# A fused linear-attention and ELU-MLP kernel: order of ScalarE work at the end of the first unit, and plain products in the second unit's first pairs

## The chip, the cores and the metric

The kernel runs on one core of a Trainium2 chip. A core has a matrix engine (TensorE, PE), three engines for elementwise work (VectorE, DVE; ScalarE, ACT; GpSimd, POOL), and SyncE (SP), which issues most transfers. Each engine works through its own instruction list in order and waits at semaphores for the others. The metric is device microseconds of one execution; the median of three timed runs counts.

## The reference

Two stages are computed in float32. The first is a gated linear attention: for each of 4 batches and 8 heads a state of 48 by 48 is decayed and updated at each of 768 positions, and the output is the query times the state. The second is a two-layer MLP with an ELU over all 3072 tokens; d_model is 384 and d_ff 2048.

```python
f = 1.0 / (1.0 + np.exp(-f_logit))
for t in range(S):
    state = f[:, :, t, :, None] * state + np.einsum('bhd,bhe->bhde', k[:, :, t], v[:, :, t])
    y[:, :, t] = np.einsum('bhd,bhde->bhe', q[:, :, t], state)
h = x @ w_in                                   # x: y with the heads side by side
g = np.where(h > 0.0, h, np.exp(np.minimum(h, 0.0)) - 1.0)
return g @ w_out
```

The weights arrive as float64 and are brought to float32 on the chip.

## The kernel before, in words

The tokens are cut into 12 *units* of 256 (`U`); d_ff is cut into 8 *pairs* (`NP`) of two 128-wide tiles. A program step is numbered `T`; there are 16 steps in a unit, two in a pair. In an even step `up(P)` forms the hidden activations of pair P, and in an odd step `down(P - LAG)`, two pairs behind, multiplies the finished activations by `w_out` and adds them up in PSUM. P counts through all units, so pairs 0 to 7 belong to unit 0, and pairs 8 to 15 to unit 1. What else happens in a step (attention of later units, weights, blends) is registered with `at_step(T, ...)` and emitted before the step's `up` or `down`; `later` holds work emitted at the end of a step. The whole order is written out by hand, so each engine's list is the order in which the Python code emits instructions. This driver is the loop at the end of `fast`, and the registrations stand just before it.

Unit 0 is *direct*: `up` is 6 matmuls of 256 columns into one PSUM buffer of the tag "h" (L946), and `down` 4 matmuls of 384 columns (L978). From unit 1 on (`m >= DIRECT`) both are Strassen-like products of 2 by 2 blocks with seven block products in place of eight. `up7` (L901) takes two "h" buffers, `pa` and `pb`; there are two in all. Its combined weights are made by `mix` (L882) and its combined inputs by `blend` (L889), both on POOL. `down` needs sums of the activations, four POOL operations for each pair, made in `elu` (L965), and differences of `w_out` blocks, `combos`, made by the generator `combine` on VectorE (L869), one operation for each step from step `CB` on; its matmuls are 192 columns wide (L1003). At the end of a unit VectorE puts four PSUM banks together into the output (L1013, L1014).

The ELU of a direct pair: `exped` has ScalarE do Relu and Exp from PSUM (L933, L934); `elu` has VectorE do the rest (L955), still reading the pair's PSUM buffer, which is free only after that. For a seven-product pair ScalarE copies one block (`u1`, L908), VectorE adds it to two others (L910, which frees `pa`), and `joined` does three further adds (L923, which free `pb`) before Relu and Exp.

Weights: part n arrives in one of seven slots of `area`, VectorE splits it (`split`, L567, L571), ScalarE lowers the lower half (`lower`, L577), and VectorE merges both into float32 (`merge`, L585). Parts 14 and 15 are the last two parts of `w_out`. `combos` lie in slots of `area` that have been emptied by then.

Attention of unit 2: `gates(2)` (L616, L618) is two ScalarE operations over the forget gates; `decays` (L630 scan, L635 reciprocal, both on VectorE, then scaling by POOL at L625) follow in steps 16, 18 and 20, and `settle` in step 22. `warm(0, "a0", MORE)` emits `MORE` matmuls of one by one element (L1058) in step 22. Unit 0's result is copied from PSUM to SBUF by ScalarE (L985) in step 19; unit 1's `down` writes over the same banks from step 21 on.

Of the kernel before, what the change touches and what calls it, by code (L numbers as in the profile page):

```python
# [17 lines left out]
def general(  # L18
# [38 lines left out]
    PAD = 64 - D  # L57
    LAG = 2
    HALF = (slice(0, D), slice(64, 64 + D))
# [297 lines left out]
def fast(ctx: ExitStack, tc: tile.TileContext, q, k, v, f_logit, w_in, w_out, out, flag, outer):  # L357
# [30 lines left out]
    NFT = DFF // 128  # L388
    NKT = DM // 128
    PAD = 64 - D  # L390
    NP = NFT // 2
    DH = DM // 2
    DIRECT = 1
    LAG = 2
    AHEAD = 7
    WA = 1
    F1 = 3
    W0 = 3
    SMALL = 16
    MORE = 5  # L400
    RR = 2
    HOLD = 2
    A1 = (2, 8, 10, 11)
# [3 lines left out]
    A3 = (2, 5, 9, 11)  # L407
    BL = 13
    MX = 10
    CB = 16  # L410
    BL1 = 13
    LIMIT = 2.0**80

# [103 lines left out]
    if wide:  # L517
        combos = [area[:, i].bitcast(FP32).rearrange("p (n f) -> p n f", f=DH) for i in (5, 6, 0, 1)]
    else:
        apart = cst.tile([128, 4, NP, DH], FP32, name="combos")  # L520
        combos = [apart[:, i] for i in range(4)]
# [7 lines left out]
    order = [divmod(i, NP) for i in range(NU * NP)]  # L529
# [3 lines left out]
    needs = sorted(  # L533
        (2 * P + out_ * (2 * LAG + 1), j, out_) for P, (m, j) in enumerate(order) if m == 0 for out_ in range(2)
    )
# [37 lines left out]
    def lower(n):  # L573

        if wide and n < NFT:
            raw = raws[n]
            nc.scalar.activation(raw.bitcast(U16)[:, 2::4], raw.bitcast(U32)[:, 0::2], AF.Copy, scale=2.0**-29)  # L577
# [33 lines left out]
    def gates(u, pieces=(NKT,), bias=1):  # L611

        p = 0
        for n in pieces:
            a = qkf[u % NB]["f"][:, p : p + n, 0]
            nc.scalar.activation(a, a, AF.Exp, scale=-1.0)  # L616
            if bias:
                nc.scalar.activation(a, a, AF.Copy, bias=1.0)  # L618
            p += n
# [210 lines left out]
    plan, later = {}, {}  # L830

    def at_step(step, *todo):
        plan.setdefault(step, []).extend(todo)
# [25 lines left out]
    gs, ss, pms, phs = {}, {}, {}, {}  # L859

    def combine():

        b = [[wo[:, i::2, h * DH : (h + 1) * DH] for h in range(2)] for i in range(2)]
        t = combos
        for n in range(0, NP, 2):
            for to, x, y in (
                (t[0], b[0][1], b[0][0]), (t[1], b[1][1], t[0]), (t[2], b[1][1], b[0][1]), (t[3], b[1][0], t[1]),
            ):
                nc.vector.tensor_tensor(  # L869
                    out=to[:, n : n + 2], in0=x[:, n : n + 2], in1=y[:, n : n + 2], op=ALU.subtract  # L870
                )
                yield
# [18 lines left out]
    def up7(P):  # L891
# [19 lines left out]
        add(h[:, 0:2], pa[:, 1:3], u1[:].unsqueeze(1).broadcast_to([128, 2, 128]))  # L911
        if order[P - 1][0] >= DIRECT:
            elu(P - 1)
# [23 lines left out]
    def up(P):  # L937

        m, j = order[P]
        if m >= DIRECT:  # L940
            up7(P)
# [10 lines left out]
    def elu(P):  # L952
        m, j = order[P]
        g = gs[P]
        nc.vector.scalar_tensor_tensor(  # L955
            out=g[:], in0=g[:], scalar=-1.0, in1=phs.pop(P), op0=ALU.add, op1=ALU.max
        )
        if m >= DIRECT:
            s = ss[P] = sb.tile([128, 4, 128], FP32, tag="sums", name=f"sums{m}_{j}", bufs=3)
            a = [[g[:, i, t * 128 : (t + 1) * 128] for i in range(2)] for t in range(2)]  # L960
            for i, x, y, op in (
                (0, a[1][0], a[1][1], ALU.add), (2, a[0][0], a[1][0], ALU.subtract),
                (1, s[:, 0], a[0][0], ALU.subtract), (3, a[0][1], s[:, 1], ALU.subtract),
            ):
                nc.gpsimd.tensor_tensor(out=s[:, i], in0=x, in1=y, op=op)  # L965
# [3 lines left out]
    def down(P):  # L969
        m, j = order[P]  # L970
        if j == 0:
            pms[m] = [ps.tile([128, DM], FP32, tag=f"m{i + (m < DIRECT)}", name=f"psM{m}_{i}") for i in range(NW if m < DIRECT else 4)]
        pm, g = pms[m], gs.pop(P)
        ends = dict(start=(j == 0), stop=(j == NP - 1))
        if m < DIRECT:
            for i in range(2):
                for t in range(NW):
                    nc.tensor.matmul(  # L978
                        pm[t][:], lhsT=g[:, i, t * 128 : (t + 1) * 128], rhs=wo[:, 2 * j + i, :],
                        start=(j == 0 and i == 0), stop=(j == NP - 1 and i == 1),  # L980
                    )
            if j == NP - 1:
                o = (outer if (NU - m) % 2 else sb).tile([128, 2, DM], FP32, tag="o", name=f"o{m}", bufs=1)
                for t in range(NW):
                    nc.scalar.copy(o[:, t], pm[t][:])  # L985
                    t0 = m * U + t * 128
                    nc.sync.dma_start(out=out[t0 : t0 + 128, :], in_=o[:, t])
                del pms[m]
            return
        s = ss.pop(P)  # L990
        a = [[g[:, i, t * 128 : (t + 1) * 128] for i in range(2)] for t in range(2)]
        b = [[wo[:, 2 * j + i, h * DH : (h + 1) * DH] for h in range(2)] for i in range(2)]
        c = [combos[i][:, j] for i in range(4)]

        todo = [
            (0, 0, a[0][0], b[0][0]), (3, 0, a[0][1], b[1][0]), (0, 1, s[:, 1], c[1]),
            (1, 0, s[:, 0], c[0]), (1, 1, s[:, 2], c[2]), (2, 1, a[1][1], c[3]), (2, 0, s[:, 3], b[1][1]),
        ]
        if j == 0:
            todo = todo[3:] + todo[:3]  # L1000
        for bank, half, x, y in todo:
            first = j == 0 and (bank, half) in ((0, 0), (3, 0), (1, 0), (2, 1))
            nc.tensor.matmul(  # L1003
                pm[bank][:, half * DH : (half + 1) * DH], lhsT=x, rhs=y,
                start=first, stop=(j == NP - 1), skip_group_check=True,
            )
        if j == NP - 1:
            p = [[pm[i][:, h * DH : (h + 1) * DH] for h in range(2)] for i in range(4)]
            o = (outer if (NU - m) % 2 else sb).tile([128, 2, DM], FP32, tag="o", name=f"o{m}", bufs=1)
            u2 = sb.tile([128, DH], FP32, tag="u2", name=f"u2_{m}", bufs=1)  # L1010
            u43 = sb.tile([128, 2, DH], FP32, tag="u43", name=f"u43_{m}", bufs=1)
            flat = o[:].rearrange("p t f -> p (t f)")
            add = lambda to, x, y: nc.vector.tensor_tensor(out=to, in0=x, in1=y, op=ALU.add)  # L1013
            (nc.vector.tensor_copy if m == NU - 1 else nc.scalar.copy)(u2[:], p[0][0])  # L1014
            add(flat[:, 0:DH], p[3][0], u2[:])
            add(u2[:], p[0][1], u2[:])
            add(u43[:], pm[1][:].rearrange("p (h f) -> p h f", h=2), u2[:].unsqueeze(1).broadcast_to([128, 2, DH]))
            add(flat[:, 3 * DH :], p[1][0], u43[:, 1])
            add(flat[:, DH : 3 * DH], pm[2][:], u43[:].rearrange("p h f -> p (h f)"))
            def store(*queues):  # L1020
                for t in range(2):
                    for h in ((1, 0) if t else (0, 1)):
                        queues[t].dma_start(
                            out=out[m * U + t * 128 : m * U + (t + 1) * 128, h * DH : (h + 1) * DH],
                            in_=o[:, t, h * DH : (h + 1) * DH],
                        )

            if m == NU - 1:
                left.append(store)
            else:  # L1030
                store(nc.sync, nc.sync)
            del pms[m]
# [70 lines left out]
    a = qkf[1]["f"][:, 0:NKT, 0]  # L1103
# [36 lines left out]
    scale(1, ("q", 1, nc.gpsimd), ("q", 2, nc.gpsimd))  # L1140
    at_step(A1[2], lambda: outputs(1), lambda: lower(A1[2]), lambda: lower(A1[2] + 1))
    for n in range(1, NFT):
        t = min(max(needs[n][0] - 2, 0), n)
        at_step(t, lambda n=n: merge(n))
        if n > 1:
            later.setdefault(max(t - 2, 0), []).append(n)
    at_step(F1, lambda: move(1, 1, nc.scalar))
    at_step(F1 + 2, lambda: scale(1, ("q", NKT, nc.gpsimd)))
    at_step(A1[0], lambda: transposed(1, 0, "a0"), lambda: transposed(1, 1, "a1"))
# [1 line left out]
    at_step(22, lambda: warm(0, "a0", MORE))  # L1151
    attention(1, (), A1)
    at_step(8, lambda: load(2))
    at_step(14, lambda: gates(2))
    attention(2, D2, A2)
    weights = combine()
    for n in range(NFT):
# [5 lines left out]
    for u in range(3, NU):  # L1163
        t = (u - 1) * NFT
# [5 lines left out]
    for n in range(NR):  # L1170
        t = 3 * NFT + (NU - 4) * NFT * n // NR + RR
# [4 lines left out]
    for T in range(NU * NFT):  # L1176
        P = T // 2
        sevens = order[P][0] >= DIRECT
        if T % 2 and sevens:
            joined(P)  # L1180
        if T % 2 == 0 and P and order[P - 1][0] < DIRECT:
            elu(P - 1)
        for f in plan.pop(T, ()):
            f()
        if T % 2 == 0:
            up(P)
        elif P >= LAG and T not in joint:
            if T - 2 in joint:
                down(P - LAG - 1)
            down(P - LAG)  # L1190
        for n in later.pop(T, ()):
            split(n)
            if n not in (A1[2], A1[2] + 1):
                lower(n)
    elu(NU * NP - 1)
    for P in range(NU * NP - LAG, NU * NP):
# [51 lines left out]
```

## Time and profile before

| what | value |
|---|---|
| three runs | 562.26, 562.70, 563.56 us; median 562.7 |
| profiled execution | 563.12 us, of which the span from first to last instruction is 561.4 |
| TensorE busy | 542.9 us, 97% of the span |
| TensorE weight loads | 507.9 us, 90% |
| VectorE busy | 407.5 us, 73% |
| ScalarE busy | 228.1 us, 41% |
| GpSimd busy | 293.3 us, 52% |
| mean granted TensorE clock | 0.995 of full speed |

All times of a trace are counted from the span's start. A matmul in float32 appears as two records, each with its own weight load; records overlap, so the distance from start to start tells the rate rather than the duration. A line of a timeline gives start, duration of the stretch, engine, line of the code, operation, output and inputs, shapes and the count; in square brackets stands the idle time before it and what ended it. In a list of waits, a line gives who waited, for whom, and then the sum in us, the number of times and the longest.

### The profile page before, as it was taken

To read this page: it belongs to the slowest core of one execution; us is meant where nothing else is said; L and a number is where in the kernel's file an instruction comes from. 1 tells how busy PE (TensorE), PEld (TensorE's weight loads), DVE (VectorE), ACT (ScalarE), POOL (GpSimd) and SP (SyncE) were. 2 spreads that over 40 slices of the span, in tenths; PEclk is the share of its full clock that TensorE was granted. 3 is DMA by queue.
4 is the path that set the end of the run, shared out by engine and by line. 5 is a ranking of instruction groups with operands and counts; after the bars stand their busy time and mean duration, and the time that the engine had idled before them with its cause. 6 is when DMAs were issued, how large, how long until landed. Compare 5 with 4: busy or idle time off the path is not lost.

```text
span 561.4 us, 15627 instructions
## 1 busy us (share of the span) xinstructions
PE 542.9 (97%) x6358; PEld 507.9 (90%) x6358; DVE 407.5 (73%) x804; ACT 228.1 (41%) x442; POOL 293.3 (52%) x567
## 2 busy tenths in 40 slices
PE   6889989999999999999999999999999999999996
PEld 2466768999999999999999999999999999999995
DVE  8888989786675785785785785786687777735553
ACT  3288752443343434434344343343333343333331
POOL 6600797475375375465366267257258348325332
PEclk9999989999999999999999999999999999999999
DMA  8999971024025216207307307207307302301101
GB/s 198 233 266 247 276 184 43 3 48 123 2 48 149 61 26 182 77 18 189 81 9 189 87 10 190 85 9 191 86 9 185 93 9 71 87 5 33 31 2 34
DMA packets 39474, 54.30 MB, mean 97 GB/s; under 512 B 4032, under 2 KB 29216, under 8 KB 39392
## 3 DMA queue, kind: packets, MB, share of 16 engines
q1 hardware_dynamic: 38592, 52.61, 36.3%
q8 instruction: 52, 0.85, 0.6%
q10 hardware_dynamic: 800, 0.59, 0.5%
q14 instruction: 30, 0.25, 0.2%
HBM read 45.02 MB, written 4.72 MB: 89 GB/s over the span
## 4 chain that ended last, share of the span: by engine, by line
PE 85%; DMA 7%; DVE 3%; ACT 2%; issue 1%; SPq 1%; POOL 0%; ACTq 0%; DVEq 0%; POOLq 0%
PE psH L901 39%; PE psM L1003 36%; DMA area<-in_moe_w_in_dram 5%; DMA area<-in_moe_w_out_dram 2%; PE psY L751 2%; PE psY L771 2%; PE psU_a L736 2%; PE psS L713 2%; ACT area L577 1%; PE psT L673 1%; PE psM L978 1%; DVE bits L567 1%; DVE gg L955 0%; DVE wi L585 0%; DVE state L694 0%
## 5 line engine op out<-in xcount | busy, mean ns | idle before, releaser
L901 PE MATMUL psH<-xt,wi 128*128 128x128 f32 (+1 forms) x1056 | 195.9, 295 | 0.0
L965 POOL TENSOR_TENSOR sums<-gg 128x128 f32<-128x128 f32 x176 | 77.6, 462 | 209.6 <-DVE gg L955 190.9
L933 ACT ACTIVATE gg<-hh 128x512 f32<-128x512 f32 x88 | 55.5, 631 | 252.9 <-DVE hh L923 111.9
L901 PEld LDWEIGHTS psH<-xt,wi 128*128 128x128 f32 x1056 | 150.1, 192 | 1.6
L901 PE MATMUL psH<-xt,area 128*128 128x128 f32 x704 | 122.0, 275 | 2.0 <-DVE gg L955 2.0
L901 PEld LDWEIGHTS psH<-xt,area 128*128 128x128 f32 x704 | 106.9, 192 | 6.8 <-DVE gg L955 2.2
L910 DVE TENSOR_TENSOR hh<-psH,u 128x256 f32<-128x256 f32 x88 | 37.0, 421 | 99.6 <-ACT u L908 99.6
L1003 PE MATMUL psM<-area,sums 128*128 128x192 f32 x528 | 102.1, 326 | 0.1
L1003 PEld LDWEIGHTS psM<-area,sums 128*128 128x128 f32 x528 | 88.0, 190 | 0.2 <-issue 0.2
L1003 PE MATMUL psM<-wo,gg 128*128 128x192 f32 x352 | 73.9, 332 | 0.0
L955 DVE SCALAR_TENSOR_TENSOR gg<-gg,hh 128x512 f32<-128x512 f32 x88 | 63.3, 720 | 1.5 <-ACT gg L934 1.5
L635 DVE RECIPROCAL f<-f 128x256 f32<-128x256 f32 x36 | 62.8, 1747 | 1.1
L934 ACT ACTIVATE gg<-gg 128x512 f32<-128x512 f32 x96 | 60.5, 631 | 3.0
L1003 PEld LDWEIGHTS psM<-wo,gg 128*128 128x128 f32 x352 | 56.3, 190 | 1.4
L923 DVE TENSOR_TENSOR hh<-psH,u43h 128x256 f32<-128x256 f32 (+1 forms) x176 | 54.7, 353 | 3.0
L965 POOL TENSOR_TENSOR sums<-gg,sums 128x128 f32<-128x128 f32 x88 | 46.8, 532 | 6.9
L625 POOL TENSOR_TENSOR q<-q,f 128x256 f32<-128x256 f32 x48 | 39.7, 829 | 18.1 <-DMA area<-in_moe_w_in_dram 15.1
L625 POOL TENSOR_TENSOR k<-k,f 128x256 f32<-128x256 f32 x48 | 39.7, 830 | 9.5 <-DMA f<-f 6.7
L923 DVE TENSOR_TENSOR u43h<-psH,hh 128x256 f32<-128x256 f32 x88 | 37.0, 421 | 9.2 <-PE psH L901 8.5
L965 POOL TENSOR_TENSOR sums<-sums,gg 128x128 f32<-128x128 f32 x88 | 43.4, 493 | 0.0
L1003 PE MATMUL psM<-area,gg 128*128 128x192 f32 x176 | 43.0, 326 | 0.0
L1003 PE MATMUL psM<-wo,sums 128*128 128x192 f32 x176 | 43.0, 326 | 0.0
(100 smaller groups left out, 648.7 us busy)
## 6 DMA issues: line engine op xcount, KB each, us to landing
area<-in_moe_w_out_dram SPq DMA_DIRECT2D x8, 768.0 KB, 11.0
again<-in_moe_w_in_dram SPq DMA_DIRECT2D x16, 384.0 KB, 4.2
again<-in_moe_w_out_dram SPq DMA_DIRECT2D x16, 384.0 KB, 3.7
k<-in_k_dram SPq DMA_DIRECT2D x12, 384.0 KB, 4.5
q<-in_q_dram SPq DMA_DIRECT2D x12, 384.0 KB, 5.6
v<-in_v_dram SPq DMA_DIRECT2D x12, 384.0 KB, 6.0
area<-in_moe_w_in_dram SPq DMA_DIRECT2D x8, 576.0 KB, 9.4
out_dram<-o SPq DMA_DIRECT2D x42, 96.0 KB, 2.0
```

The lines of the kernel that those rows point to most:

```text
L625: e.tensor_tensor(out=t[n][:, p], in0=t[n][:, p], in1=t["f"][:, p, "kq".index(n)], op=ALU.mult)
L635: nc.vector.reciprocal(f[:, p, 1], f[:, p, 0])
L713: nc.tensor.matmul(pc[r][FULL[b], w, p], lhsT=t["k"][FULL[r], p, cols], rhs=t["q"][FULL[r], p, cols], start=True, stop=True,)
L736: nc.tensor.matmul(pu[b][FULL[r], w, p], lhsT=kn[FULL[b], p, w, FULL[r]], rhs=vs[u % NB][FULL[b], w, PAD + h * D : PAD + (h + 1) * D], sta ...
L901: nc.tensor.matmul(to, lhsT=lhs, rhs=rhs, start=(n == 0), stop=True, skip_group_check=True)
L910: add = lambda to, x, y: nc.vector.tensor_tensor(out=to, in0=x, in1=y, op=ALU.add)
L923: add = lambda to, x, y: nc.vector.tensor_tensor(out=to, in0=x, in1=y, op=ALU.add)
L933: nc.scalar.activation(g[:], h, AF.Relu, scale=-1.0)
L934: nc.scalar.activation(g[:], g[:], AF.Exp, scale=-1.0)
L955: nc.vector.scalar_tensor_tensor(out=g[:], in0=g[:], scalar=-1.0, in1=phs.pop(P), op0=ALU.add, op1=ALU.max)
L965: nc.gpsimd.tensor_tensor(out=s[:, i], in0=x, in1=y, op=op)
L1003: nc.tensor.matmul(pm[bank][:, half * DH : (half + 1) * DH], lhsT=x, rhs=y, start=first, stop=(j == NP - 1), skip_group_check=True,)
```

## The change

- Step 15 gets `elu` of pair 7, then `gates(2)`, then `lower` of part 15. Before, `gates(2)` was in step 14 ahead of `up(7)`, `lower(15)` at the end of step 13, and `elu(7)` at the start of step 16. Since `up(7)` emits its Relu and Exp in step 14, these now stand ahead of the gates and of the last lowering in ScalarE's list.
- `merge` of part 15 goes from step 15 to step 17; its `split` stays in step 13.
- Pairs 0 to 3 of unit 1 (`PLAIN`) have no sums; their `down` is eight plain products of 192 columns, into halves of PSUM banks 3 and 2. Pair 4 opens banks 0 and 1, and pairs 4 to 7 use seven products. One further addition at the end of unit 1 brings in the half bank that the plain products filled.
- `combine` starts in step 20, not 16, and makes the combinations of pairs 4 to 7 first and those of pairs 0 to 3, which unit 2 is first to use, afterwards.
- `MORE` goes from 5 to 1.

```diff
+    PLAIN = 4
-    MORE = 5
+    MORE = 1
-    CB = 16
+    CB = 20
...
-        for n in range(0, NP, 2):
+        for n in (*range(PLAIN, NP, 2), *range(0, PLAIN, 2)):
...
-        if m >= DIRECT:
+        if m > DIRECT or m == DIRECT and j >= PLAIN:
             s = ss[P] = sb.tile([128, 4, 128], FP32, tag="sums", name=f"sums{m}_{j}", bufs=3)
...
+        plain = PLAIN if m == DIRECT else 0
+        if j < plain:
+            alone = ((3, 0), (2, 0)), ((2, 1), (3, 1))
+            todo = [(*alone[t][h], a[t][i], b[i][h]) for i in range(2) for t in range(2) for h in range(2)]
+            starts = ((3, 0), (2, 0)) if j == 0 else ()
+        else:
+            s = ss.pop(P)
+            c = [combos[i][:, j] for i in range(4)]
+            todo = [
+                (0, 0, a[0][0], b[0][0]), (3, 0, a[0][1], b[1][0]), (0, 1, s[:, 1], c[1]),
+                (1, 0, s[:, 0], c[0]), (1, 1, s[:, 2], c[2]), (2, 1, a[1][1], c[3]), (2, 0, s[:, 3], b[1][1]),
+            ]
+            if j == plain:
+                todo = todo[3:] + todo[:3]
+            starts = ((0, 0), (3, 0), (1, 0), (2, 1)) if j == 0 else ((0, 0), (1, 0)) if j == plain else ()
+        started = set()
         for bank, half, x, y in todo:
-            first = j == 0 and (bank, half) in ((0, 0), (3, 0), (1, 0), (2, 1))
+            first = (bank, half) in starts and bank not in started
+            started.add(bank)
...
             add(flat[:, 3 * DH :], p[1][0], u43[:, 1])
+            if plain:
+                add(flat[:, 3 * DH :], p[3][1], flat[:, 3 * DH :])
...
-        t = min(max(needs[n][0] - 2, 0), n)
+        t = min(max(needs[n][0] - 2, 0), n) + 2 * (n == NFT - 1)
         at_step(t, lambda n=n: merge(n))
         if n > 1:
-            later.setdefault(max(t - 2, 0), []).append(n)
+            later.setdefault(max(min(t, n) - 2, 0), []).append(n)
...
-    at_step(14, lambda: gates(2))
+    at_step(15, lambda: elu(NP - 1), lambda: gates(2), lambda: lower(NFT - 1))
...
-        if T % 2 == 0 and P and order[P - 1][0] < DIRECT:
+        if T % 2 == 0 and 0 < P < NP:
             elu(P - 1)
...
-            if n not in (A1[2], A1[2] + 1):
+            if n not in (A1[2], A1[2] + 1, NFT - 1):
                 lower(n)
```

## The prediction

> **What bounds the kernel now.** First the shares by engine, then what TensorE waited for, then the timelines round its longest wait.
>
> ```profile
> PE 542.9 (97%) x6358; PEld 507.9 (90%) x6358; DVE 407.5 (73%) x804; ACT 228.1 (41%) x442; POOL 293.3 (52%) x567
> PE psH L901 <- DVE gg L955: 2.0, 1, 2.0
> ```
>
> TensorE is the bound; from the second unit on nothing counts but its own work and its few waits. The waits before 60 us belong to the start, which the change leaves alone. After that one long wait is left, a single one of 2.0 us. TensorE's timeline (start, us, line, operation, count; in brackets idle time and releaser):
>
> ```profile
> 74.75 0.39 PE L901 MATMUL psH<-xt,wi 128*128 128x128 f32 x2
> ...
> 77.78 0.84 PE L901 MATMUL psH<-xt,area 128*128 128x128 f32 x4 [1.98 <-DVE gg L955]
> ...
> 80.55 3.29 PE L978 MATMUL psM<-wo,gg 128*128 128x384 f32 x8
> 83.68 0.38 PE L901 MATMUL psH<-xt,wi 128*128 128x128 f32 x2
> ...
> 86.12 2.75 PE L978 MATMUL psM<-wo,gg 128*128 128x384 f32 x8
> 88.70 0.39 PE L901 MATMUL psH<-xt,wi 128*128 128x128 f32 x2
> ```
>
> At 74.75 the first seven-product pair (pair 8: unit 1's first) begins. Its second PSUM buffer is the one that pair 7's direct product occupies until `elu` (L955) has read it. ScalarE says why that is late:
>
> ```profile
> 72.36 1.99 ACT L577 ACTIVATE area<-area 128x768 uint16<-128x768 uint32 x1
> 74.09 0.90 ACT L616 ACTIVATE f<-f 128x768 f32<-128x768 f32 x1
> 75.02 0.84 ACT L618 ACTIVATE f<-f 128x768 f32<-128x768 f32 x1
> 75.77 0.58 ACT L933 ACTIVATE gg<-psH 128x512 f32<-128x512 f32 x1
> 76.38 0.63 ACT L934 ACTIVATE gg<-gg 128x512 f32<-128x512 f32 x1
> ```
>
> Pair 7's product is complete about 72.2 (its 12 records start at 69.58, the next line's at 72.17), but its Relu waits behind the last `lower` and both `gates`: 3.4 us. VectorE's L955 then runs from 77.04 and TensorE resumes at 77.78. The windows of one us (length, PE busy, clock, DMA) show a second cost:
>
> ```profile
> 77.00:78.00 1.00, 0.22 (x2) 1.00 1.16 212
> 78.00:79.00 1.00, 1.00 (x7) 0.61 1.11 239
> 79.00:80.00 1.00, 1.00 (x5) 0.50 1.15 251
> 80.00:81.00 1.00, 1.00 (x5) 0.50 1.14 251
> 81.00:82.00 1.00, 1.00 (x3) 0.68 1.09 265
> 82.00:83.00 1.00, 1.00 (x4) 1.00 0.71 195
> ```
>
> Right after the wait the clock is halved for 0.78 + 1 + 1 + 0.64 = 3.42 us, so 1.7 us more is lost. Wait and slow clock together: the stretch 74.75 to 83.68 is one seven-product `up` and one direct `down`, 8.93 us; the next such stretch, 83.68 to 88.70, takes 5.02. **The episode costs 3.91 us.**
>
> **What the Trainium skill says.** "TensorE: Matmul & The Clock Gate", Part 1: TensorE's activity is judged in free-running windows of 3413 ns, and an idle window halves the clock. The trace agrees on length (3.42 us) but was stricter than "idle": 74.80 to 78.20 was busy for 1.42 of 3.40 us. Free-running also means that a 2 us wait need not cost the same in every execution. Same page, "Architectural detail": ScalarE and VectorE are strict FIFO; that is what the Relu shows above. "PSUM — Partial Sum Buffer", "The four PSUM rules": a first matmul clears the accumulate bits of its whole bank, so a bank may be opened only once; no run here shows it yet, and the new `starts` lists open banks 3 and 2 at pair 0 and banks 0 and 1 at pair 4.
>
> **The change part by part.** Sums are against the profiled execution: 563.12 us, span 561.4 and 1.72 around it. That lies 0.42 above the median 562.7, inside the three runs' 1.3 us.
>
> *Exponentials first.* On ScalarE the order becomes: lower(14), Relu(7), Exp(7), gates(2) twice, lower(15), copy u1 of pair 8. Lower(14) ends 72.4; Relu and Exp at 0.6 each end 73.6; `elu(7)`, now in step 15, goes behind merge(14) (72.68 + 1.12), so about 73.75 to 74.4. TensorE wants the buffer at 74.75 + 0.89 (83.68 to 84.57 in the undisturbed pair) = 75.64. It has 1.2 us to spare: the wait and its slow clock go, −3.91. Blend's POOL results for the same matmuls end about 76.2, for a product due at 76.31: hidden, just.
>
> *What is late next.* Gates end 75.25, lower(15) 77.1, u1(8) 77.3, against 77.17 before. VectorE: scan and reciprocal of unit 2 (0.94 + 1.75) from 75.35 to 78.0, then hh(8) to 78.35, the three adds of pair 8 to 79.45, merge(15), moved here, to 80.5. TensorE asks for these buffers at 74.75 + 5.02 = 79.77 and 80.66: 1.4 and 1.2 us spare. Had the first combinations (0.49 to 1.00 each, four in steps 16 to 19) stayed, most of that would be gone. Next: scan and reciprocal to 83.2, hh(9) 83.5, elu(8) 84.2, adds(9) 85.3; wanted 84.79 and 85.68. Spare 0.4. Then Relu and Exp(9) to 86.65 and the two output copies of unit 0 (L985, 0.84 for both) to 87.4: plain `down(8)`, at 87.23, writes bank 3 first and bank 2 at 87.56, which the second copy frees. Spare 0.15. Then hh(10) 88.8 and adds(10) 90.6 against 89.92 and 90.81. Spare 0.2. None waits by this sum, but three margins are thinner than my reading of sequential gaps, so I put in +0.2, with bounds 0 and 1.0. From step 24 VectorE has caught up (before it idled 2.74 us there).
>
> *Plain pairs.* Seven matmuls of 192 columns become eight. The rows of 14 records step by 2.28 us (4.72 less 2.44 of `up`), so 0.163 a record, two records a matmul: 0.326 each, four pairs, +1.30. It is on the path. As a check: sixteen such records make 2.61, and the direct `down` of unit 0, eight records of 384 columns, steps by 88.70 − 86.12 = 2.58, so loading each weight tile twice costs nothing visible. Sixteen POOL operations (about 0.46 each) and their waits vanish from pairs 8 to 11; POOL is at 52%, worth nothing by itself.
>
> *Combinations in steps 20 to 35, pairs 4 to 7 first.* Sixteen operations still, off the path. Pair 4's are ready by step 23, wanted in step 29; pairs 0 and 1 by 31, wanted in 37. Steps 20 to 31 carry no more than before; steps 32 to 35 gain about 2.3 us of VectorE work where it idled 2.85 and 1.63. Zero; without that cover up to 0.7 each. The added output sum is 0.37 at the end of unit 1, before a `down` that starts two steps later: zero.
>
> *Small matmuls 5 to 1.* Ten records cost 93.83 − 93.42 = 0.41; eight fewer save about 0.26. Merge(15) at step 17 is wanted by `down(7)` in 19: 80.5 against 82.2, zero. SP's order of transfers is unchanged.
>
> Sum: 563.12 − 3.91 + 1.30 − 0.26 + 0.2 = 560.45; the scores' 0.29 gap at 105.2 (waiting for VectorE's states) may close too, so **560.3 us**, 0.4% below the median.
>
> **Rivals.**
> *Gain partly eaten.* A new wait of 1 to 2 us at pairs 9 to 11 behind VectorE's reciprocals or the copies of L985, without a slow clock. For: margins of 0.15 to 0.4. Against: a delay shows only past them. 560.3 + 1.5 = 561.8: within 0.2%. The same result comes if the timed runs of before mostly escaped the slow clock; then less than 3.91 was there to win.
> *Slower.* ScalarE is FIFO: u1(8) now stands behind lower(15), hh(8) behind u1. If this chain, or adds(9), comes over 1.7 us late in one window, the clock halves again: 560.3 + 2 + 1.7 = 564.0. It decides once the 1.4 us spare at pair 9 is overdrawn by about 2, or the 0.4 at pair 10. Against: every term has a measured duration, and VectorE has shed four operations there.
> *The change does not do what it says.* Another release (blend, 76.2) holds pair 8: then only 0.6 of the 2.1 us remains as a wait, no slow clock, 560.9.
>
> **How the numbers follow.** Chances: main case 0.70 (own range 559.4 to 561.3, from the 0 to 1.0 of waits, the 0.3 gap and run scatter), blend 0.04, partly eaten 0.13, slower 0.13. A difference under 0.2% (561.6 to 563.8) can't be told from none. The main case and blend give nearly all of faster, 0.73; partly eaten is mostly the same, 0.12; slower, 0.15, adds a little for a stall I have not named. The range 559.3 to 562.9 leaves out the slower case and some 0.05 at the edges.
>
> **What would show it.** TensorE's list has no wait on L955 in pair 8, the clock stays 1.0 from 74 to 84, `down(8)` starts about 87.2 instead of 91.14, pair 12 about 95.7 instead of 99.31, and later stages come 2.7 us early. Wrong would be: waits at L901 or L1003 between 79 and 93, a halved window there, or a unit period other than the 43.19 between the joint steps (141.51, 184.69, 227.88 in the chain).

## The result and the profile after

| | runs | median, us | lowest to highest |
|---|---|---|---|
| before | 20 | 562.70 | 560.71 to 565.13 |
| changed | 20 | 559.86 | 557.62 to 562.28 |

The ratio is 0.9951, 95% interval 0.9937 to 0.9966: 2.8 us faster. The forecast was 560.3, which is 2.4 below the median of before.

The profile after is of the slowest of the 20 runs (562.28 us), so its span (560.5) must not be set beside that of before. Its shares by engine:

```profile
PE 543.8 (97%) x6358; PEld 508.6 (91%) x6358; DVE 406.2 (72%) x805; ACT 228.0 (41%) x442; POOL 286.3 (51%) x551
```

The list of TensorE's waits between 76 and 104 us has no line at all: the 2.0 us at L901 for L955 are gone, and nothing has replaced them. The granted clock is 1.00 in every window from 66 to 110 us. TensorE's timeline over pair 8 and the two pairs behind it (columns as in the prediction):

```profile
77.64 0.38 PE L902 MATMUL psH<-xt,wi 128*128 128x128 f32 x2
...
78.53 0.61 PE L902 MATMUL psH<-xt,area 128*128 128x128 f32 x4
...
80.08 2.75 PE L979 MATMUL psM<-wo,gg 128*128 128x384 f32 x8
82.66 0.38 PE L902 MATMUL psH<-xt,wi 128*128 128x128 f32 x2
...
90.12 2.77 PE L1013 MATMUL psM<-wo,gg 128*128 128x192 f32 x16
92.82 0.19 PE L1070 MATMUL psW<-ident 128*1 128x1 f32 x2
92.94 0.49 PE L902 MATMUL psH<-xt,wi 128*128 128x128 f32 x2
...
98.74 0.38 PE L902 MATMUL psH<-xt,wi 128*128 128x128 f32 x2
```

The second group of pair 8 now follows the first in 0.89 us (77.64 to 78.53), and pair 9 comes 5.02 us after pair 8 (82.66), not 8.93. Pair 11 begins at 92.94 and pair 12 at 98.74. ScalarE shows why:

```profile
75.26 0.60 ACT L934 ACTIVATE gg<-psH 128x512 f32<-128x512 f32 x1 [1.23 <-PE psH L947]
75.89 0.63 ACT L935 ACTIVATE gg<-gg 128x512 f32<-128x512 f32 x1
76.43 0.83 ACT L617 ACTIVATE f<-f 128x768 f32<-128x768 f32 x1
77.28 0.84 ACT L619 ACTIVATE f<-f 128x768 f32<-128x768 f32 x1
78.03 1.92 ACT L578 ACTIVATE area<-area 128x768 uint16<-128x768 uint32 x1
```

ScalarE waits for TensorE now, and no longer the other way round: Relu starts as soon as pair 7's product is there, and gates and lowering come behind it.

Yet pair 8 begins 2.89 us *later* than in the profile of before (77.64 against 74.75), in a part of the program where TensorE does the same in both kernels. Windows of one us of the changed kernel (length, PE busy with records, clock, DMA share, GB/s):

```profile
57.00:58.00 1.00, 0.29 (x2) 1.00 1.07 303
58.00:59.00 1.00, 0.95 (x49) 0.77 1.04 227
59.00:60.00 1.00, 1.00 (x25) 0.50 1.10 228
60.00:61.00 1.00, 1.00 (x3) 0.50 1.11 185
61.00:62.00 1.00, 1.00 (x4) 0.53 0.97 263
```

In this execution the half clock fell behind another wait, at 56.0 to 57.6 us, for states of unit 1's attention. In the other profiles of the same kernel pair 8 starts at 73.62 and 73.78. I therefore compare stretches counted from pair 8. In the kernel before they begin at 74.75, and pair 12 stands here:

```profile
99.31 0.38 PE L901 MATMUL psH<-xt,wi 128*128 128x128 f32 x2
```

| profile | pair 8 to pair 12 | pair 8 to the end of the span |
|---|---|---|
| before | 24.56 | 486.6 |
| changed (three profiles) | 21.10, 21.11, 21.09 | 482.9, 482.7, 483.1 |
| order only | 23.95 | 486.1 |
| plain pairs only | 22.96 | 484.5 |
| order and plain pairs, combinations early | 23.04 | 485.1 |
| before, wait filled | 24.12 | 486.1 |

By the durations in the prediction, the work in "pair 8 to pair 12" without a wait is 20.65 us for the kernel before (24.56 − 3.91) and 21.04 for the changed one (two plain pairs, 0.65 more; eight small records, 0.26 less). So in this stretch the changed kernel stands within 0.1 us of no wait at all, by this estimate.

### The profile page after: what moved, and what is told of

Its sections match the earlier page's. It is cut to its first block, busy times and chain, and to the rows that moved or that the text cites. A ratio compares the mean times of both kernels' runs of the same rounds, so it can differ in the third digit from the quotient of the medians.

```text
span 560.5 us, 15607 instructions
## 1 busy us (share of the span) xinstructions
PE 543.8 (97%) x6358; PEld 508.6 (91%) x6358; DVE 406.2 (72%) x805; ACT 228.0 (41%) x442; POOL 286.3 (51%) x551
## 4 chain that ended last, share of the span: by engine, by line
PE 90%; DMA 6%; DVE 2%; POOL 1%; issue 0%; SPq 0%; DVEq 0%; POOLq 0%
PE psH L902 39%; PE psM L1013 37%; PE psM L979 3%; PE psH L947 3%; DMA area<-in_moe_w_out_dram 2%; PE psY L752 2%; PE psY L772 2%; PE psU_a L737 2%; PE psS L714 2%; DMA area<-in_moe_w_in_dram 2%; PE psT L674 1%; DMA f<-f 1%; DMA k<-in_k_dram 1%; POOL k L626 0%; DVE wi L586 0%
## 5 line engine op out<-in xcount | busy, mean ns | idle before, releaser
L966 POOL TENSOR_TENSOR sums<-gg 128x128 f32<-128x128 f32 x168 | 73.7, 460 | 203.6 <-DVE gg L956 183.6
L1013 PE MATMUL psM<-area,sums 128*128 128x192 f32 x504 | 97.5, 326 | 0.1
L1013 PEld LDWEIGHTS psM<-area,sums 128*128 128x128 f32 x504 | 84.0, 190 | 0.2 <-issue 0.2
L1013 PE MATMUL psM<-wo,gg 128*128 128x192 f32 x400 | 81.7, 332 | 0.0
L1013 PEld LDWEIGHTS psM<-wo,gg 128*128 128x128 f32 x400 | 64.0, 190 | 1.4
L966 POOL TENSOR_TENSOR sums<-gg,sums 128x128 f32<-128x128 f32 x84 | 44.2, 527 | 6.6
L966 POOL TENSOR_TENSOR sums<-sums,gg 128x128 f32<-128x128 f32 x84 | 41.9, 499 | 0.0
L1013 PE MATMUL psM<-area,gg 128*128 128x192 f32 x168 | 41.0, 326 | 0.0
L1013 PE MATMUL psM<-wo,sums 128*128 128x192 f32 x168 | 41.0, 326 | 0.0
```

Source lines behind the costliest of these rows:

```text
L1013: nc.tensor.matmul(pm[bank][:, half * DH : (half + 1) * DH], lhsT=x, rhs=y, start=first, stop=(j == NP - 1), skip_group_check=True,)
```

## The experiments

The theory of the prediction: the wait at pair 8 and its slow clock are the gain. The rival: relief of VectorE and GpSimd. All ratios are against runs of the kernel before on the same chip.

### Only the order

```diff
-    at_step(14, lambda: gates(2))
+    at_step(15, lambda: elu(NP - 1), lambda: gates(2), lambda: lower(NFT - 1))
```

(with merge(15) and `elu` moved as in the change; all pairs with seven products, combinations from step 16, five small matmuls)

> The kernel before with only the new order: pair 7's Relu and Exp ahead of the gates, elu, gates and the last lowering in step 15, merge(15) in step 17; all pairs of unit 1 keep seven products, combinations still start in step 16, five small matmuls. Theory (the wait at pair 8 and its slow clock are the gain): the wait at pair 8 goes, but VectorE, which still makes four combinations in steps 16 to 19, is late for pair 10: by the sum of durations adds(9) end about 87.0 for a buffer wanted at 85.7, so a new wait of 1 to 2 us at pairs 9 to 11. Time 560.7 to 561.7, faster than before by 1 to 2 us. Rival (relief of VectorE and GpSimd by plain pairs and later combinations is the gain): within 0.2% of 562.7.

Measured: 562.53 us over 22 runs, ratio 1.0002 (0.9989 to 1.0015). My theory's number missed; the rival's held. TensorE's waits from 74 to 100 us:

```profile
PE psH L901 <- DVE hh L923: 0.9, 2, 0.5
PE psH L901 <- DVE hh L910: 0.6, 1, 0.6
PE psH L901 <- POOL xt L889: 0.3, 1, 0.3
```

The wait for L955 is gone, and waits for VectorE's adds have come, which hold up pairs 10 and 11:

```profile
86.26 0.49 PE L901 MATMUL psH<-xt,wi 128*128 128x128 f32 x2 [0.56 <-DVE hh L910]
...
87.94 0.68 PE L901 MATMUL psH<-xt,area 128*128 128x128 f32 x4 [0.52 <-DVE hh L923]
...
94.37 0.68 PE L901 MATMUL psH<-xt,area 128*128 128x128 f32 x4 [0.34 <-DVE hh L923]
```

The loss is more than the list says, because some of it shows only as stretched records: pair 8 to 12 took 23.95 us against 20.65 of work, 3.3 us, hardly less than the 3.5 to 3.9 of the kernel before. Of these 3.3 us, 0.5 lie at pair 8, where GpSimd's blend is late (pair 8 to 9 takes 5.54 us, not 5.02). The other 2.8 lie between pairs 9 and 12. Most of them stand behind VectorE, but not all: the weight loads of pair 8's `down` also waited 0.5 us for GpSimd's sums.

VectorE tells most of the rest. From 75.90, when it gets the gates, to 99.37 it was busy for 23.12 of 23.47 us; in the kernel before, from pair 7's `elu` on (77.04 to 99.52), for 21.88 of 22.48:

```profile
77.04:99.52 22.48, 21.88 (x36) 0.92 0.40 91
```

```profile
75.90:99.37 23.47, 23.12 (x36) 1.00 0.48 113
```

```profile
78.16:99.50 21.34, 18.78 (x32) 1.00 0.45 103
```

(before, order only, changed; length, VectorE busy, clock, DMA.) So there were two bounds in a row. In steps 16 to 22 of the kernel before, the one gap of VectorE that the timeline notes is of 0.25 us:

```profile
95.79 0.42 DVE L910 TENSOR_TENSOR hh<-psH,u 128x256 f32<-128x256 f32 x1 [0.25 <-ACT u L908]
```

Ending the wait at pair 8 only brings TensorE sooner to buffers that VectorE still holds. The new order even makes VectorE's list longer there. In the kernel before, merge(15) ran at 74.38, while VectorE was waiting for pair 7; with the new order it stands behind pair 8's adds:

```profile
80.52 1.05 DVE L585 CUSTOM_DVE_ANT_0 wo<-area,bits 128x1536 uint16<-128x1536 uint16 x1
```

Counted from pair 8, VectorE starts unit 2's first scan 2.0 us sooner than before (0.93 us after pair 8 began, not 2.90), and merge(15) takes about 1.0 of them back.

### Only the plain pairs and later combinations

```diff
-    at_step(15, lambda: elu(NP - 1), lambda: gates(2), lambda: lower(NFT - 1))
+    at_step(14, lambda: gates(2))
```

(against the changed kernel; lower(15), elu(7) and merge(15) back as well)

> The changed kernel with the old order: gates in step 14, lower(15) at the end of step 13, elu(7) at the start of step 16, merge(15) in step 15; plain pairs, later combinations and one small matmul kept. Theory: the wait of 2 us at pair 8 stays as before, and with it the chance of a slow clock; 1.30 more of matmuls and 0.26 less of small ones come on top: 563.2 to 564.2, slower by about 1 us. Rival (relief is the gain): about 560 to 561.

Measured: 561.96 us over 22 runs, ratio 0.9989 (0.9977 to 1.0000). Both forecasts missed: 1.2 us below mine at its low end, 1 us above the rival's. The waits from 74 to 104 us are one line:

```profile
PE psH L902 <- DVE gg L956: 1.6, 1, 1.6
```

The first wait stays, the waits behind VectorE are gone. The experiment with the filled wait, below, shows that the kernel before pays such waits too once the slow clock doesn't hide them. Shedding them gave back about what the plain pairs' matmuls cost, or a little more: the interval ends at 1.0000.

### The wait filled, nothing else

```diff
+        if P == NP:
+            warm(0, "m3", 30)
         products(
             (pb[:, 0], t[0], x[:, 1]), (pb[:, 2], t[2], x[:, 7]), (pb[:, 3], a[1][1], x[:, 9]),
```

> The kernel before with 30 one-by-one matmuls added between pair 8's two groups of products, about 1.9 us at 0.064 each, so that TensorE is not idle while it waits for VectorE's elu(7); they compute nothing that is used. Theory: pair 8's second group still starts about 77.8 (within 0.3), so nothing of the 2 us is won; but if such small matmuls count as activity, the clock isn't halved after this wait and the median falls by up to 1.7 us times the share of executions that lost it there, 0.5 to 1.5: about 561.7. If they don't count, 562.7 and the slow clock still appears at times. Rival (the slow clock has nothing to do with this wait): 562.7, and the slow window keeps its place.

Measured: 562.52 us over 22 runs, ratio 0.9995 (0.9984 to 1.0006). TensorE's timeline:

```profile
73.47 0.38 PE L901 MATMUL psH<-xt,wi 128*128 128x128 f32 x2
...
74.46 1.64 PE L1060 MATMUL psW<-ident 128*1 128x1 f32 x60
76.54 0.71 PE L901 MATMUL psH<-xt,area 128*128 128x128 f32 x4 [0.44 <-DVE gg L957]
```

The second group starts 3.07 us after pair 8, as before (3.03), and the clock in this profile is full from the start to 557 us, when the last matmuls are over. But the time did not move. In the waits from 72 to 100 us stand VectorE's adds, as in "only the order":

```profile
PE psH L901 <- DVE hh L925: 0.6, 2, 0.4
PE psH L901 <- DVE gg L957: 0.4, 1, 0.4
```

Pair 8 to 12 took 24.12 us with a full clock and 24.56 with 3.42 us of half clock. Of the 1.77 us that the slow clock cost TensorE, all but 0.44 was time in which it would have waited for VectorE. This rests on two profiles, one of each kernel. The median alone wouldn't show it: how often the timed runs lose the clock at pair 8 can't be read from them, since they give only a mean clock for the whole span, and that hardly differs (0.9960 over 61 runs of before, 0.9962 over the 22 with the wait filled; by estimate 0.2 us less at half clock in 560). By the same means the change itself isn't a gain of clock: 0.9961 over 104 runs of before and 0.9965 over 33 of the changed kernel, by estimate 0.2 us of TensorE's time out of 2.8.

### The combinations early again

The new theory: two bounds in a row, which only both edits together remove.

```diff
-    CB = 20
+    CB = 16
```

> The changed kernel with the combinations starting in step 16 again (still those of pairs 4 to 7 first). New theory (the wait at pair 8 and VectorE's chain of steps 16 to 22 are two bounds in a row, and only both together give the gain): four combinations, 0.5 to 1.0 us each in the trace of the kernel before, about 2.6 in all, fall back between the scans and reciprocals. Adds(9) have 0.9 us to spare in the changed kernel, adds(10) 1.1, so waits of about 1.0 at pair 10 and 0.5 at pair 11 return: about 1.5 us slower than the changed kernel, 561.4. Rival (plain pairs relieve GpSimd, and that is what counts): same as the changed kernel.

Measured: 561.71 us over 19 runs, ratio 0.9989 (0.9977 to 1.0001), 2.2 us above the changed kernel on the same chip (559.53; 1.5 expected). The waits for VectorE came back, both at pair 10:

```profile
PE psH L902 <- DVE hh L911: 0.7, 1, 0.7
PE psH L902 <- DVE hh L924: 0.5, 1, 0.5
```

```profile
85.21 0.49 PE L902 MATMUL psH<-xt,wi 128*128 128x128 f32 x2 [0.66 <-DVE hh L911]
...
86.90 0.68 PE L902 MATMUL psH<-xt,area 128*128 128x128 f32 x4 [0.53 <-DVE hh L924]
```

Pair 11, for which 0.5 us had been expected, lost only 0.1. Pairs 8 to 12 took 23.04 us, 1.9 more than in the changed kernel. Four operations of VectorE in steps 16 to 19 undo most of the change.

### The sums kept

```diff
-        if m > DIRECT or m == DIRECT and j >= PLAIN:
+        if m >= DIRECT:
```

(the four sums of each plain pair are made on GpSimd and dropped)

> The changed kernel, but the plain pairs still make their four sums on GpSimd, which nothing reads. Theory: GpSimd has room, so the same time as the changed kernel within 0.2%. Rival (relief of GpSimd): its sixteen operations delay the scaling of unit 2's keys and queries and the weight mixes, 1 us or more slower.

Measured: 560.02 us over 14 runs, ratio 0.9957 (0.9943 to 0.9972) against 0.9948 (0.9928 to 0.9969) for the changed kernel; no wait of TensorE between 70 and 110 us. The rival's 1 us or more did not come: the medians differ by 0.5 us, within the intervals, and pair 8 to 12 takes 21.24 us, not 21.10. So how much GpSimd has to do isn't what counts. One thing isn't tested: no matmul reads the sums here, so the 0.5 us that TensorE waited for them in "only the order" can't come up. For pairs 10 and 11 "two plain pairs" tests it; for pairs 8 and 9 no run does, because without plain pairs their combinations, made from step 20 on, would be wanted in step 21.

### Small matmuls

```diff
-    MORE = 1
+    MORE = 5
```

> The changed kernel with five small matmuls in step 22 instead of one. Theory (they are TensorE time, nothing else): 0.26 us more than the changed kernel, about 560.1. Rival (they cover a wait for pair 10's adds): no difference.

Measured: 560.30 us over 8 runs, ratio 0.9962 (0.9936 to 0.9989). The step is in the right direction, but 0.26 us can't be told from none by this interval.

### Two plain pairs

Since VectorE's list decides and the plain pairs only cost matmuls, two should do: pair 10's combinations are then made in steps 20 to 23 and wanted in step 25.

```diff
-    PLAIN = 4
+    PLAIN = 2
```

> The changed kernel with two plain pairs instead of four; combinations still from step 20, in the order pairs 2 to 7, then 0 and 1, so VectorE's list in steps 16 to 22 is the same. Theory (VectorE's list decides, plain pairs only cost matmuls): two matmuls fewer, 0.65 us faster than the changed kernel, about 559.2. Rival (GpSimd's sums of pairs 10 and 11 come too late for their products): no gain, with waits at the products of pair 10 or 11.

> The changed kernel once more, on the same chip as the other three, for comparison: 0.9951 of the kernel before within its interval. Its profile should show no wait of TensorE between pairs 8 and 12: 21.1 us from the start of pair 8 to the start of pair 12, wherever the slow clock falls.

Measured: 558.70 (6 runs, 0.9937, 0.9915 to 0.9958) against 559.53 for the changed kernel (6 runs, 0.9948, 0.9928 to 0.9969). The intervals overlap, so both were run once more, with a third kernel that also drops the last small matmul (`warm` in step 22 removed):

> Two plain pairs instead of four once more, beside the changed kernel on the same chip, since six runs left the difference inside both intervals. Theory: 0.4 to 0.65 us faster than the changed kernel (the earlier traces show 0.43 between pair 12 and the end of unit 1). Rival: equal within 0.1%.

> Two plain pairs, and no small matmul in step 22. Theory (small matmuls are only TensorE time, adds(10) have about 1 us to spare): 0.1 us less than with two plain pairs and one small matmul, not to be told by the times; the trace shows no wait at pair 11. Rival (it covers a wait): a wait appears at pair 11.

> The changed kernel, for comparison on the same chip: 0.995 of the kernel before, no wait between pairs 8 and 12.

Measured: two plain pairs 558.89 (0.9931, 0.9909 to 0.9954); no small matmul besides 558.40 (0.9931, 0.9907 to 0.9956); changed kernel 559.32 (0.9945, 0.9924 to 0.9965). None of the three profiles with two plain pairs has a wait of TensorE between 70 and 110 us. Two plain pairs came out 0.8 and 0.4 us below the changed kernel, the same way on both occasions; the stretch from pair 12 to pair 20, by which unit 1 is done, is 0.43 us shorter in the trace (46.02 against 46.45). Against the kernel before it is clearly faster, by 0.6 to 0.7%; against the changed kernel likely so, though each difference alone lies within the intervals. The rival (GpSimd's sums too late) shows nowhere. Dropping the last small matmul makes no difference that the times tell, and no wait appears at pair 11.

## Why the prediction was right, step by step

**Pair 8's wait.** Right, to the digit: pair 8 to pair 9 went from 8.93 to 5.02 us, the 3.91 of the sum. `elu(7)` ended 0.40 us before pair 8 even began (77.24 against 77.64); I had 0.35.

```profile
76.55 0.69 DVE L956 SCALAR_TENSOR_TENSOR gg<-gg,psH 128x512 f32<-128x512 f32 x1 [1.15 <-ACT gg L935]
```

**What 3.91 was.** Here the reading was wrong, though the sum held. "Wait and slow clock" were booked as two losses of 2.1 and 1.8. The filled wait shows that the second was nearly empty: with a full clock the kernel before loses 24.12 − 20.65 = 3.47 us between pairs 8 and 12, 2.2 at pair 8 and 1.3 behind VectorE at pairs 10 and 11. The 1.8 of slow clock should have been 1.3 of VectorE's lateness. The prediction had the clue in its own "What is late next" (had the first combinations stayed, most of the spare time would be gone) and used it only for the changed kernel; the later combinations it booked at zero. "The combinations early again" shows that 1.9 us of the gain between pairs 8 and 12 hang on them. So the sum held partly by luck: the same change took away a second bound that the sum didn't have. That VectorE had next to no gap from 77.04 to 99.52 was there to be read in the timeline of before.

**What is late next.** Right in kind and half a us too gloomy. In the profile after, adds(9) end at 87.66 and are wanted at 88.57, 0.9 spare (I had 0.4); adds(10) end at 92.7 for 93.93, 1.2 spare (0.2); the copies end at 89.82 for 90.45, 0.6 spare (0.15). The 0.2 us of waits that I added did not come.

**Plain pairs.** Sixteen records in 2.60 us (96.14 to 98.74); 2.61 forecast. But pair 11's extra 0.33 lies ahead of unit 2's attention products, which in the kernel before wait for ScalarE and VectorE in their midst: from pair 13 to pair 14 TensorE needs 7.62 us now and 8.03 before, 0.74 less than with the extra matmuls. So one of the four pairs cost nothing and 0.4 was won besides. I had only the 0.29 gap before the scores, of which 0.1 closed.

**Small matmuls.** 2.61 after 90.12 is 92.73; pair 11 begins at 92.94. They take 0.21 now and 0.41 before: 0.20 saved, 0.26 forecast.

**The sum from pair 8 on**, in the two profiles: −3.91 + 0.65 − 0.20 to pair 12, +0.23 to pair 13 and −0.42 from there to pair 20, and −0.08 after it: −3.73, where the sum of the prediction has −3.91 + 1.30 − 0.26 + 0.2 − 0.15 = −2.8 (to 560.3 from 563.12). The medians moved by 2.8. That the medians agree better with my sum than the profiles do is partly luck: the profile of before lost 0.4 us more than the filled one, and the start of the program moves by some us from execution to execution (pair 8 began between 73.1 and 77.6 us in the profiles). The unit period, which the prediction named as a sign, stayed at 43.2 us. The profiles moved by 3.7 us and the medians by 2.8; the half us that is left after those 0.4 stays open.

**The rivals.** "Partly eaten" and "slower" named the right place (VectorE's reciprocals and adds at pairs 9 to 11). It is what the order alone does, and the combinations early: 2 to 3 us, without a slow clock in those pairs. In the change they didn't occur because four combinations had left steps 16 to 19. The third rival, GpSimd's blend holding pair 8, doesn't show in the three profiles of the changed kernel (pair 8 to 9 takes 5.02 or 5.03 us in each). But the margin, "just" hidden, was read rightly as thin: with the order alone pair 8 to 9 takes 5.54 us, with five small matmuls 5.40, with two plain pairs and no small matmul 5.22, and with the sums kept 5.17, with no slow clock in that stretch. Each time the first product with a blended input starts late; the waits name the blend in the first two.

## What to carry to other kernels

When the bound engine has one visible wait, ask what it would meet next if that wait were gone. A supplier that has next to no gap for the 20 us behind it (VectorE here: 21.88 of 22.48 us busy) may be the second bound, and then ending the first wait alone gains nothing. Here the experiments say so: order alone 1.0002, relief alone 0.9989, both 0.9951. And slow-clock time is not all to be won: here, by two profiles, some of it covered waits that then came to light.

## What the runs showed of the hardware that was not expected

The half clock follows no fixed place in the program: it fell behind the wait at 75.8 us in the profile of before and behind that at 56.0 us in the profile after. With the order alone it came at 28.9 us, with the plain pairs alone at 27.0 us, where it lasted 6.8 us, and in the other nine profiles nowhere before the last matmuls. In the first two it lasted about 3.4 us each time, and the 3.4 us just ahead of it were busy for 1.42 us in the first and 1.70 us in the second. "TensorE: Matmul & The Clock Gate" of the Trainium skill, Part 1, speaks of an idle window as what brings the half clock; here the stretch ahead was not idle, but 42% and 50% busy. Sixty records of one-by-one matmuls (1.64 us in all), put into a wait of 2.2 us, stood in the one profile taken with a full clock after it; one profile does not show that they caused it.
